# Top-k attention and a low-rank mixer on one core: rounding passes spread over the fills, transposes of the second batch moved, an inverse moved

## The chip, the cores and the metric

One core of one Trainium2 chip. The metric is the device time of one execution in microseconds (us). The core has five engines with a queue each, which work through their instructions in order and wait for each other by semaphores: TensorE (PE, with its weight loads PEld), VectorE (DVE), ScalarE (ACT), GpSimd (POOL) and SyncE (SP), which issues the transfers.

## The reference

Attention over 8 batches x 8 heads, 576 rows, 64 columns a head; in each row of scores only the 32 largest stay. Its output, put together over the heads, goes through a mixer: a low-rank mix over the rows and a two-layer product over the channels.

```python
scores = scale * np.matmul(q, k.transpose(0, 1, 3, 2))
kth = np.partition(scores, -top_k, axis=-1)[..., -top_k:-top_k + 1]
scores = np.where(scores >= kth, scores, -1000000000.0)
attn = np.exp(scores - np.max(scores, axis=-1, keepdims=True))
attn = attn / (np.sum(attn, axis=-1, keepdims=True) + 1e-09)
x = np.matmul(attn, v)                    # then to (8, 576, 512)
h = x.transpose(0, 2, 1) @ U @ V
u = x + h.transpose(0, 2, 1)
out = u + np.maximum(u @ w_ch1, 0.0) @ w_ch2
```

U, V and the two weight matrices come in 64-bit floats; the kernel makes 32-bit ones of them on the chip.

## The kernel before

**Pairs and steps.** Two heads of a batch are a pair: 4 pairs a batch, 32 in all. A pair's 576 rows are cut into four blocks of 128 rows (for both heads, in two "chunks" of 576 scores) and a tail of 64 rows (both heads in one chunk). A block is a step: 5 steps a pair, 20 a batch, 160 in all, numbered n = 0 to 159, with g = n // 5 the pair and t = n % 5 (t = 4 is the tail). The order on PE, ACT, DVE and POOL is written out by hand: what the Python loop issues first stands first in the queue.

**What happens to one block.** `scores` (L271) makes the scores on PE and ACT copies them to `Ssb` (L305 to L307, three buffers). `front` (L327) is a generator that is moved on by `next`: four rounds on DVE find the 32 largest (L346 the first eight, then L356 blanks what was found and L360 finds eight more; a step begins with L346). Then the chunk is masked and `E = exp` is made, on one of three ways (`ways`, L314):

- early: ACT makes exp before the mask, DVE masks and sums with L366;
- pooled: POOL makes a mask (L363) and adds it to the scores (L364), then ACT makes exp with its sum (L312);
- gaps: ACT makes a relu of the distance to the least kept score (L380, L381), POOL subtracts it (L382), then ACT makes exp (L312).

In batches 0 and 1 (pairs 0 to 7) a step has a gaps chunk and, but for tails, a pooled chunk; `eased` says so. Those steps take three `next(last)` in the step after. From pair 8 on there is an early and a pooled chunk. The end of batch 0 (pair 3) has its own ways.

`turns` (L391) transposes a block's `E` on PE: four transposes of the first chunk, four of the second (L402), one for the last columns (L407), each group into a buffer `tp` and copied by ACT to `PT` (L403, L408). There are two `tp` buffers, shared with all other short PE results (`O`, `pT`, `up`, the transposes of q, k and of the output). `values` (L417) multiplies with v into `O`; ACT copies it to `XT` (L448). The sums `den` are inverted on DVE (L414, L415) by `inverse` (L411).

**The mixer.** When a pair is complete, `mixed` (L451, a generator too) turns `XT` back (L460), ACT copies it (L464), POOL multiplies with the inverted sums (L465); after `wait` further fills PE makes `pT` (L471), ACT copies `Tb`, and PE makes `up` (L483, L485), which ACT copies into `uT` (L493). After the last pair of a batch it appends that batch's products, `mlp(b)` (L498), to `fillers`. Over the eight batches these are 1024 products on each of two lines, each product in two passes on PE: L508 from `uT` to `hT` (ACT's relu L520), L527 from `hT` to the output columns, of which ACT makes `oT` (L542), POOL adds `uT` (L543), PE turns it back (L555), and SP stores it. The last of these turns is issued as soon as the batch's products run out (L546).

**Fills.** The products of a batch are dealt out over the 20 steps that follow. `fill` (L582) moves `mixing` on by one, adds a share to `due` and issues products until `due` is used up; if there are none, `due` is set to 0. A step has 8 fills. In batch 0 there is nothing to fill in; what is left at the end runs alone.

**The weights.** 36 layers of raw 64-bit words are loaded by `next_params` (L205). For each, ACT runs three passes over the raw words (L165, L167, L168: Copy with a scale, Identity with a scale and bias, Sign); at the call after, DVE shifts (L175) and POOL adds twice (L176, L178). A call joins the layer of the call before, runs the passes of the next, and starts a load. It is called up to twice a step, until about step 28.

## Time and profile before

| | us |
|---|---|
| median of 4 runs | 1846.93 (1846.5 to 1847.78) |
| the profiled execution, its own time | 1846.5 |
| its span, first to last instruction | 1843.7 |
| PE busy | 1740.1 (94%), 10528 matmuls |
| DVE busy | 1570.6 (85%) |
| ACT busy | 1015.4 (55%) |
| POOL busy | 684.4 (37%) |
| products on PE, L508 and L527 | 557.1 and 562.3 |
| DVE's rounds, L346, L356, L360 | 205.0, 211.7 + 427.7, 614.7 |

Spans and waits are from the profiled execution. A line of a timeline gives the start, the duration, the engine, the source line, the operation with the tiles it writes and reads, and in brackets how long its engine sat idle before it and what released it. A line of the list of waits gives the waiting engine and line, what it waited for, and then the total in us, the number of times and the longest. Since the kernel changes its bottleneck on the way (DVE alone in batch 0, products on PE beside attention after that, products alone at the end), the busy shares are read by stretches.

### The profile page before, as it was taken

How to read it: one execution, taken by the hardware profiler on the slowest of the kernel's cores; microseconds unless marked ns; L12 is line 12 of the kernel's file. 1: busy time of each engine (PE TensorE's matmuls, PEld its weight loads, DVE VectorE, ACT ScalarE, POOL GpSimd, SP SyncE). 2: the span in 40 equal slices, each digit the busy share in tenths (PEclk: the TensorE clock that was granted, in tenths of full speed). 3: DMA queues.
4: the chain of work that ended last, by engine and by line, in shares of the span. 5: the costliest groups of instructions: out<-in, count | busy, mean ns of one | idle time of the engine just before them, and what ended most of it. 6: DMA issues, size and time to landing. Idle time of an engine off the chain costs nothing.

```text
span 1843.7 us, 29145 instructions
## 1 busy us (share of the span) xinstructions
PE 1740.1 (94%) x10528; PEld 1316.8 (71%) x10528; DVE 1570.6 (85%) x3208; ACT 1015.4 (55%) x2518; POOL 684.4 (37%) x471
## 2 busy tenths in 40 slices
PE   4656889999999999999999999999999999999999
PEld 2344656787778877787777877788777877778677
DVE  7999998999999999998999999999999999996000
ACT  5787777665546555555555555555555555454110
POOL 4777577453333223423233233323223333332000
PEclk7777899999999999999999999999999999999999
DMA  4232221101010000111010010110001010000000
GB/s 109 78 89 84 66 77 47 31 24 29 20 28 23 22 20 20 32 25 31 15 27 17 24 29 21 30 25 24 19 17 31 21 32 19 10 8 7 6 15 12
DMA packets 127294, 58.20 MB, mean 32 GB/s; under 512 B 89904, under 2 KB 124976, under 8 KB 127152
## 3 DMA queue, kind: packets, MB, share of 16 engines
q1 hardware_dynamic: 126096, 56.10, 11.5%
q8 instruction: 83, 1.36, 0.3%
q14 instruction: 59, 0.48, 0.1%
q10 hardware_dynamic: 1056, 0.26, 0.1%
HBM read 46.89 MB, written 9.44 MB: 31 GB/s over the span
## 4 chain that ended last, share of the span: by engine, by line
PE 84%; DVE 10%; POOL 3%; ACT 2%; issue 1%; DMA 0%; SPq 0%; POOLq 0%; DVEq 0%; ACTq 0%
PE mm L508 26%; PE mm L527 26%; PE sc L294 7%; PE O L439 6%; PE tp L402 6%; DVE rr L356 4%; DVE m L360 3%; PE sc L281 2%; PE O L426 2%; PE up L483 2%; PE O L436 1%; DVE first L346 1%; PE tp L266 1%; PE tp L555 1%; PE up L485 1%
## 5 line engine op out<-in xcount | busy, mean ns | idle before, releaser
L360 DVE MAX8 m<-rr 128x8 f32<-128x576 f32 x864 | 614.7, 748 | 5.5
L527 PE MATMUL mm<-hT,w 128*128 128x256 f32 (+1 forms) x2048 | 562.3, 410 | 0.0
L508 PE MATMUL mm<-uT,w 128*128 128x256 f32 (+1 forms) x2048 | 557.1, 410 | 1.8 <-ACT hT L520 1.8
L363 POOL TENSOR_SCALAR E<-Ssb,m 128x576 f32<-128x576 f32 x127 | 284.0, 2236 | 564.1 <-DVE m L360 405.9
L508 PEld LDWEIGHTS mm<-uT,w 128*128 128x128 f32 x2048 | 363.4, 190 | 108.3 <-issue 27.6
L527 PEld LDWEIGHTS mm<-hT,w 128*128 128x128 f32 x2048 | 360.5, 190 | 97.7 <-issue 22.5
L356 DVE MATCH_REPLACE8 rr<-m,rr 128x576 f32<-128x576 f32 x576 | 427.7, 742 | 0.0
L403 ACT COPY PT<-tp 128x512 f32<-128x512 f32 x288 | 168.4, 587 | 127.2 <-PE tp L402 126.2
L312 ACT ACTIVATE E<-Ssb,nmax 128x576 f32<-128x576 f32 x288 | 223.0, 775 | 26.4 <-POOL Ssb L364 16.3
L346 DVE MAX8 first<-Ssb 128x8 f32<-128x576 f32 x288 | 205.0, 748 | 17.4 <-ACT Ssb L307 17.4
L356 DVE MATCH_REPLACE8 rr<-first,Ssb 128x576 f32<-128x576 f32 x288 | 211.7, 742 | 0.0
L402 PE MATMUL tp<-ident,E 128*128 128x128 f32 x1152 | 178.0, 279 | 35.4 <-ACT E L312 14.2
L402 PEld LDWEIGHTS tp<-ident,E 128*128 128x128 f32 x1152 | 141.5, 143 | 86.9 <-ACT E L312 24.6
L364 POOL TENSOR_TENSOR Ssb<-Ssb,E 128x576 f32<-128x576 f32 x127 | 179.5, 1413 | 10.6
L294 PE MATMUL sc<-qkT 64*128 64x288 f32 x1024 | 168.5, 449 | 12.0 <-ACT Ssb L305 7.9
L366 DVE SCALAR_TENSOR_TENSOR E<-Ssb,m,E 128x576 f32<-128x576 f32 x122 | 109.3, 896 | 73.5 <-ACT E L312 62.7
L520 ACT ACTIVATE hT<-mm 128x320 f32<-128x320 f32 (+1 forms) x256 | 104.2, 407 | 118.1 <-PE mm L508 117.7
L439 PE MATMUL O<-PT,va 128*64 128x128 f32 x2048 | 145.2, 286 | 0.0
L448 ACT COPY XT<-O 128x128 f32<-128x128 f32 x128 | 34.1, 267 | 176.6 <-PE O L439 176.5
L543 POOL TENSOR_TENSOR oT<-oT,uT 128x320 f32<-128x320 f32 (+1 forms) x56 | 44.5, 795 | 225.9 <-ACT oT L542 205.2
L294 PEld LDWEIGHTS sc<-qkT 64*128 64x128 f32 x1024 | 91.9, 195 | 50.2 <-issue 16.2
L439 PEld LDWEIGHTS O<-PT,va 128*64 128x64 f32 x2048 | 113.5, 141 | 16.1 <-issue 1.3
(80 smaller groups left out, 1554.9 us busy)
## 6 DMA issues: line engine op xcount, KB each, us to landing
raw<-in_moe_w_ch_dram SPq DMA_DIRECT2D x32, 512.0 KB, 3.7
va<-in_v_dram SPq DMA_DIRECT2D x64, 128.0 KB, 2.3
out_dram<-ob SPq DMA_DIRECT2D x64, 128.0 KB, 1.9
ld_q<-in_q_dram SPq DMA_DIRECT2D x63, 128.0 KB, 2.8
ld_k<-in_k_dram SPq DMA_DIRECT2D x63, 128.0 KB, 2.7
ld_ends<-in_q_dram SPq DMA_DIRECT2D x32, 32.0 KB, 2.1
ld_ends<-in_k_dram SPq DMA_DIRECT2D x32, 32.0 KB, 2.2
vd<-in_v_dram SPq DMA_DIRECT2D x64, 16.0 KB, 2.0
```

The source lines that it names most:

```text
L294: nc.tensor.matmul(sc[:, h, 0:HALF], lhsT=qkT[half(h), 0, cols(t)], rhs=qkT[half(h), 1, i * HALF : (i + 1) * HALF], start=True, stop=True,)
L312: nc.scalar.activation(E, chunk, AF.Exp, bias=nmax, scale=SCALE, accum_out=total)
L346: nc.vector.max(ms[c], curs[c])
L356: nc.vector.match_replace(nxt, ms[c], curs[c], NEG)
L360: nc.vector.max(ms[c], curs[c])
L363: nc.gpsimd.tensor_scalar(Es[c], chunks[c], ms[c][:, 7:8], NEG, ALU.is_lt, ALU.mult)
L364: nc.gpsimd.tensor_tensor(chunks[c], chunks[c], Es[c], ALU.add)
L402: nc.tensor.transpose(tp[:, j, :], E2[:, a : a + P], ident)
L403: nc.scalar.copy(PT[:, NT * h : NT * h + NT], tp)
L439: nc.tensor.matmul(O[half(h)], lhsT=va[:, h, j, :], rhs=PT[:, NT * h + j], start=False, stop=(j == NT - 1),)
L508: nc.tensor.matmul(ph[:, 0:w], lhsT=w1[:, cc, f * P : (f + 1) * P], rhs=uT[:, cc, lo:hi], start=(cc == 0), stop=(cc == NC - 1),)
L527: nc.tensor.matmul(po[:, 0:w], lhsT=w2[:, f, c * P : (c + 1) * P], rhs=hTs[f][:, 0:w], start=(f == 0), stop=(f == NF - 1),)
```

## The change

Four edits, all of them to the order in which things are issued; no instruction is added or left out.

1. `f64_parts` no longer runs ACT's three passes but puts them into a list `passes`. Each `fill` runs one, before it moves `mixing` on; what is left is run at the head of the next `next_params`.
2. At n = 19, the last step of batch 0, `inverse` is called after the tail's rounds instead of before the last two of them.
3. Where the block of step n - 1 is eased (steps 21 to 40), its first group of transposes is no longer issued at the end of step n, but with the two others in step n + 1: one after the first fill, two after the second.
4. In steps after batch 0, `mixed` waits 5 fills instead of 4.

```diff
@@ f64_parts
-        nc.scalar.activation(bits.bitcast(F32), hi.bitcast(F32), AF.Copy, scale=RESCALE)
-        lows = low.bitcast(F32)
-        nc.scalar.activation(lows, low8, AF.Identity, bias=four[0:n], scale=-(1 + 2.0**-10) * 2.0**-26)
-        nc.scalar.activation(hi.bitcast(F32), hi.bitcast(F32), AF.Sign, bias=nudge[0:n])
+        lows, his = low.bitcast(F32), hi.bitcast(F32)
+        passes.extend((
+            lambda: nc.scalar.activation(bits.bitcast(F32), his, AF.Copy, scale=RESCALE),
+            lambda: nc.scalar.activation(
+                lows, low8, AF.Identity, bias=four[0:n], scale=-(1 + 2.0**-10) * 2.0**-26
+            ),
+            lambda: nc.scalar.activation(his, his, AF.Sign, bias=nudge[0:n]),
+        ))
@@ next_params
+        while passes:
+            passes.pop(0)()
         while parts:
             f64_join(*parts.pop(0))
@@ fill
         for _ in range(k):
+            if passes:
+                passes.pop(0)()
             if mixing and next(mixing[0], True):
                 mixing.pop(0)
@@ the loop, n = 19
             if n < ALONE:
+                next(here)
+                next(here)
                 inverse(g, 0, 2 * NT)
-                next(here)
                 mixing.append(mixed(g, 1))
                 fill()
-                next(here)
                 next(here)
                 continue
@@ the loop, from n = 21 on
         next(turning, None)
         fill()
         next(turning, None)
+        if eased(*divmod(n - 2, CH)):
+            next(turning, None)
         fill()
         next(ready, None)
...
         if n - 2 >= ALONE and (n - 2) % CH == NT:
-            mixing.append(mixed((n - 2) // CH, 4))
+            mixing.append(mixed((n - 2) // CH, 5))
...
         if n <= STEPS:
             turning = turns(*divmod(n - 1, CH))
-        next(turning, None)
+        if not ease:
+            next(turning, None)
         fill()
```

## The prediction

> **What bounds the kernel now.** I read the page first, then the busy times cut at the steps of the loop (a step starts where DVE begins a new `L346`), then PE's waits in each stretch, then the timeline around every wait that this change can touch.

> The page: slices of 46 us, tenths busy.

> ```profile
> span 1843.7 us, 29145 instructions
> PE   4656889999999999999999999999999999999999
> DVE  7999998999999999998999999999999999996000
> ...
> L268 ACT ACT_TABLE_LOAD x1 | 1.3, 1283 | 2.1 <-issue 2.1
> ```

> DVE is full first, PE from slice 7 on, and the last three slices are PE alone. (The third row, from ScalarE's list of groups, is used below.) The same in stretches that end at steps 20, 30, 40 and so on; columns are PE, PEld, DVE, ACT and POOL busy, then the granted clock.

> ```profile
> 11.30:209.00 197.70, 121.99 (x744) 81.15 (x743) 192.12 (x393) 147.54 (x355) 138.36 (x101) 0.75 0.29 83
> 209.00:317.40 108.40, 97.08 (x571) 67.24 (x571) 97.78 (x199) 81.90 (x197) 78.54 (x55) 1.00 0.23 68
> 317.40:416.00 98.60, 98.60 (x643) 78.12 (x642) 89.99 (x182) 65.39 (x175) 47.31 (x31) 1.00 0.11 26
> 628.00:840.60 212.60, 211.76 (x1318) 161.73 (x1317) 197.66 (x407) 115.70 (x288) 68.79 (x44) 1.00 0.10 24
> ```

> Steps 0 to 18 are DVE's (0.07 us idle in most steps); in steps 20 to 29 PE is idle 11.3 us and DVE 10.6 us, each waiting for the other through ScalarE and GpSimd; from step 30 PE is never idle but for 0.83 us a batch. So after 317 us only PE's waits count, before it what makes PE late. PE's waits in 209 to 318 us, then in 470 to 1690 us, and DVE's in 198 to 470 us (total, times, longest):

> ```profile
> PE tp L402 <- ACT E L312: 4.8, 3, 1.9
> PE mm L508 <- ACT hT L520: 1.8, 1, 1.8
> PE pT L471 <- POOL x L465: 1.2, 1, 1.2
> ...
> PE tp L555 <- POOL oT L543: 4.1, 5, 0.8
> ...
> DVE first L346 <- ACT Ssb L307: 16.5, 6, 5.0
> DVE den L414 <- ACT E L312: 3.1, 1, 3.1
> ```

> Two places in the timeline: step 29, where DVE waits for ScalarE, ScalarE for GpSimd, and PE for ScalarE; and the end of a batch's products in step 62.

> ```profile
> 313.76 1.40 POOL L382 TENSOR_TENSOR Ssb<-Ssb,E 128x576 f32<-128x576 f32 x1
> 315.19 0.77 ACT L312 ACTIVATE E<-Ssb,nmax 128x576 f32<-128x576 f32 x1 [0.49 <-POOL Ssb L382]
> 316.11 0.66 PE L402 MATMUL tp<-ident,E 128*128 128x128 f32 x4 [1.94 <-ACT E L312]
> 317.39 1.42 DVE L346 MAX8 first<-Ssb 128x8 f32<-128x576 f32 x2 [5.00 <-ACT Ssb L307]
> ...
> 655.47 0.37 ACT L542 COPY oT<-mm 128x256 f32<-128x256 f32 x1 [0.49 <-PE mm L527]
> 655.92 0.72 POOL L543 TENSOR_TENSOR oT<-oT,uT 128x256 f32<-128x256 f32 x1 [3.60 <-ACT oT L542]
> 656.70 0.44 PE L555 MATMUL tp<-ident,oT 128*128 128x128 f32 x2 [0.83 <-POOL oT L543]
> 658.85 1.24 PE L294 MATMUL sc<-qkT 64*128 64x288 f32 x8
> ```

> **1. The passes dealt out.** The number of instructions stays (36 of each, 0.67 to 0.78 us for a full layer); only ScalarE's order changes. In steps 0 to 18 DVE waits for nothing of ScalarE's and the score copies stand almost a step ahead of their use, so I take 0. If that cover went, each step could lose up to one pass, 0.75 us. In steps 20 to 29 there are two effects. A gain: the relu that frees PE's product buffer no longer stands behind three passes; of the 1.8 us wait some 1.2 go. A loss: GpSimd's `L176` needs the third pass, and in steps 23 and 28 its order puts that pass behind an `hT` or `ob` copy. The chain L176, L178, L363, L364, L382, `L312`, `L307` that ends in DVE's 5.00 us wait then starts about 0.6 and 0.75 us later. A loss of 1.35 us on DVE's side, bounds 0 and 2 x 1.5.

> [...]

> **2. The inverse behind the rounds.** DVE's `L414` waits 3.1 us at step 19 with the tail's rounds queued behind it (`L356`, `L360`, then all of step 20). The two remaining rounds take 4 x 0.75 to 0.83 us = 3.2 us, which is when the sums are there. DVE starts step 20 at about 205.9 instead of 209.0. What waits for `den` is GpSimd's `L465`, not before 210.3, so that costs nothing. PE's chain at that place (it runs through `uT`, `O`, `PT` copies) gains only some 0.7 us, from the `uT` copy that stood behind three passes. So DVE's 3.1 us are no end gain by themselves; of them I let 2.0 reach step 29: 3.1 less the 0.6 of part 1, less 0.5 since PE, 0.7 us earlier, has only its 1.5 us wait in step 22 to give. Bounds 0 and 3.1.

> **3. The second batch's transposes.** In steps 21 to 40 the first four transposes leave the end of a step, where three of them waited 4.8 us in all for an `E` just being made, for the next step's start. But nothing DVE waits for is bought by that: its 5.00 us are ScalarE standing at `L312` for GpSimd. And the new place has its own waits. There are two buffers `tp`. The last transpose (`L407`) now follows the second four at once and takes the first four's buffer, so it needs their copy (`L403`, 0.59 us), which on ScalarE stands behind `L380` and `L381` (0.2 + 0.78 us), and those behind DVE's last round. `values` then waits for one copy more: 0.6 us later in step 29 (309.55 + 0.27 before). Before step 30: 1.94 us wait gone, less 0.6, plus the 2.0 of part 2, less 0.44 for four transposes only put off: PE is 2.9 us ahead at step 30. Bounds 0.3 and 6.5 (all three waits gone, 4.8, and 1.7 more).

> From step 30 PE is full, and each new wait counts. With a fill between, the copy has 1.0 to 1.5 us and needs about 0.9: I charge 0.1 us in ten of twelve steps. In steps 32 and 37 `up` comes directly after `L407` and needs the copy of the second four, started only as they end: 0.3 + 0.59 - 0.1 = 0.8 us each. Together 2.6 us lost; bounds 0 and 12 x 0.9 = 10.8.

> **4. `mixed` waits a fill longer.** The 1.2 us wait of `pT` goes, inside the stretch counted above. From batch 2 on nothing waited there; the new order leaves at least 0.85 us between `pT` and `up` where the copy of `Tb` ends 0.6 us after the last `pT` starts (703.7 to 704.3 us in batch 2): 0, bounds 0 and 24 x 0.2 = 4.8. Past step 42 it does something unmeant. The next batch's products are appended when `mixed` ends, one fill later; in step 42 nothing else is left, so that fill issues none. All later products slip by one fill (about 0.97 of a 512-column product, about 0.9 us of PE work, which is put off, not added). A batch's products therefore end in the fill after `values` and `scores` instead of before. The `oT` of the last rows is made at the same place; `L555` comes 1.3 + 1.24 us of PE work later. The five waits of 0.83 us have nothing left to wait for: 4.1 us gained. Bounds 0 and 5 x 1.0. One `oT` add per batch also falls behind `L363` and `L364` on GpSimd (2.2 + 1.4 us), but its reader comes most of a step later. The waits of step 42 and of the last batch (1.3 us each) stay.

> [...] Weight loads are 161.7 of 212.6 us here, which would leave room to swallow the 4.1 us; but the timeline's products start every 0.22 us (256 columns) and 0.27 us (320) without a break, so I count them.

> **Sum**, against this execution: -2.9 + 2.6 - 4.1 = -4.4 us, span 1839.3. The execution took 1846.5 us with 2.8 us around the span; the median of the four is 1846.93, so I predict **1842.5 us**. The bounds together: best -6.5 - 5 = -11.5, worst -0.3 + 10.8 + 4.8 = +15.

> **Rivals.**
> - *B, given back.* The waits of part 3 eat the start's gain, or the scores' copies on ScalarE delay `oT`, so that part 4 only moves its wait: one of the two gains stays, -1.5 to -3 us, about 1845. For it: ScalarE is in order and busy 82 of 108 us. Against: PE gets 2.5 us of work in between, where 0.83 us is missing.
> - *C, slower.* `L407`'s buffer. If the first four's copy comes 1.2 us later than I think in each of steps 30 to 41, PE loses 12 x 1.2 = 14.4 us, of which -2.9 - 4.1 pay 7.0: +7.4, 1854. It is slower at all from 0.58 us a step. Against: `L380` runs early in the step there, and ScalarE is idle 3 us a step.
> - *D, more.* DVE's and PE's waits of steps 20 to 29 go together and nothing comes back: -6.5 - 4.1 = -10.6, 1836.3.
> - That the change does not do what it says is no rival for the order (the built programs show the instructions moved as written), but the products' slip is not in its name.

> **Chances.** Forecast 0.52, B 0.20, C 0.15, D 0.13. A measurement of this kernel can tell about 0.2%, 3.7 us, from no change. My forecast lies just beyond that: 0.42 of its 0.52 is faster than 1843.2, 0.10 within. With D: faster 0.55. Within: 0.10 + B + 0.02 of C = 0.32. Slower 0.13. The range 1835 to 1851 leaves out the far ends of C and D.

> **What would show it.** Right: DVE's wait at `L414` gone and step 20 at 206; PE's waits for `E` gone; `L555` waiting twice instead of seven times; batches 212.4 us apart becoming about 211.6; DVE still idle 4 to 5 us in steps 24 and 29. Wrong: PE waits on `PT` or `Tb` copies between 318 and 430 us of more than 3 us; any PE wait in steps of batch 2 and later; a batch still taking 212.4 us.

## The result and the profile after

The changed kernel takes 1843.5 us (median of 37 runs, 1842.11 to 1844.81) where the kernel before takes 1846.76 us (median of 57 runs shown with them): 3.3 us less, a ratio of 0.9982 with a 95% interval of 0.9977 to 0.9987. The prediction was 1842.5 us. The profiled execution spans 1840.8 us where that of before spanned 1843.7. Line numbers of the changed kernel are 1 to 6 higher than those of before: `L175` is now `L179`, `L346` is `L352`, `L402` is `L408`, `L407` is `L413`, `L520` is `L526`, `L555` is `L561`.

The page of the changed kernel, span and the two rows of busy tenths in slices of 46 us:

```profile
span 1840.8 us, 29144 instructions
PE   4666889999999999999999999999999999999999
DVE  7999988989999999999999999999999999995000
```

Its busy times in the same stretches, cut at its own steps 20, 30 and 40 and at one batch (PE, PEld, DVE, ACT, POOL busy, then the granted clock, DMA share, GB/s):

```profile
11.30:205.60 194.30, 122.32 (x719) 81.20 (x718) 191.93 (x393) 145.58 (x351) 138.43 (x101) 0.72 0.30 85
205.60:315.35 109.75, 101.94 (x604) 70.92 (x603) 97.01 (x199) 83.89 (x201) 78.47 (x55) 1.00 0.22 67
315.35:415.64 100.29, 98.25 (x637) 77.31 (x636) 89.99 (x182) 65.03 (x175) 47.25 (x31) 1.00 0.10 26
627.60:839.80 212.20, 211.93 (x1320) 162.57 (x1319) 196.42 (x407) 117.32 (x290) 68.35 (x44) 1.00 0.10 24
```

Step 20 starts 3.4 us earlier (205.60, before 208.99), step 30 only 2.0 (315.35, before 317.39), step 40 0.4 (415.64, before 416.01). From there each batch of 20 steps takes 211.74 us (839.41 to 1051.15) instead of 212.37, five times 0.63.

PE's waits in 205 to 318 us (total, times, longest), those of 0.4 us and more:

```profile
PE tp L413 <- ACT PT L409: 6.2, 6, 3.0
PE tp L408 <- ACT E L318: 0.4, 1, 0.4
PE pT L477 <- ACT x L440: 0.4, 1, 0.4
PE O L442 <- ACT PT L414: 0.4, 1, 0.4
```

One of the six waits at `L413`, 0.6 us, lies in step 30 already, the other five (5.6 us) before it. PE's waits in 318 to 470 us; from 470 to 1690 us the view lists none any more, where before it listed five of 0.83 us:

```profile
PE tp L561 <- POOL oT L549: 1.3, 1, 1.3
PE up L489 <- ACT PT L409: 1.1, 2, 0.6
PE tp L561 <- ACT PT L409: 0.2, 1, 0.2
```

The waits for `E` (4.8 us before), `hT` (1.8) and `x` from GpSimd (1.2) are gone or small; in their place PE waits 6.2 us at the last transpose, `L413`, for the copy that frees its buffer. DVE's waits in 195 to 470 us: the one at the sums is gone, the one for the score copies is longer than before (19.8, before 16.5):

```profile
DVE first L352 <- ACT Ssb L313: 19.8, 8, 5.8
DVE E L372 <- ACT E L318: 3.9, 2, 2.3
DVE w L179 <- ACT w L167: 1.1, 2, 0.6
```

The longest new wait, in the timeline of step 25 (start, length, engine, what, idle before):

```profile
260.25 0.69 ACT L167 ACTIVATE w<-raw 128x512 f32<-128x512 f32 x1
260.38 0.60 PE L408 MATMUL tp<-ident,E 128*128 128x128 f32 x4
260.83 0.75 ACT L168 ACTIVATE raw<-raw,four 128x512 f32<-128x512 uint8 x1
261.48 0.75 ACT L171 ACTIVATE raw<-raw,nudge 128x512 f32<-128x512 f32 x1
262.12 0.19 ACT L386 ACTIVATE least<-m 128x1 f32<-128x1 f32 x1
262.34 0.77 ACT L387 ACTIVATE E<-Ssb,least 128x576 f32<-128x576 f32 x1
263.02 0.42 ACT L526 ACTIVATE hT<-mm 128x320 f32<-128x320 f32 x1
263.34 1.06 ACT L409 COPY PT<-tp 128x512 f32<-128x512 f32 x2
263.97 0.33 PE L413 MATMUL tp<-ident,E 128*128 128x128 f32 x1 [2.99 <-ACT PT L409]
```

ScalarE is never idle here. Ahead of the copy that PE needs stand the three rounding passes that part 1 dealt to the first fills, then `L386`, `L387` and a relu: part 1 and part 3 meet in ScalarE's queue. (Part 3 has such waits without part 1 too; see its run alone.) And the end of a batch's products, in step 62: the add is done at 657.63, the transposes start at 658.76 behind `scores`, and wait for nothing:

```profile
656.45 0.37 ACT L548 COPY oT<-mm 128x256 f32<-128x256 f32 x1 [0.49 <-PE mm L533]
656.56 0.85 PEld L445 LDWEIGHTS O<-PT,va 128*64 128x64 f32 x16
656.90 0.73 POOL L549 TENSOR_TENSOR oT<-oT,uT 128x256 f32<-128x256 f32 x1 [5.07 <-ACT oT L548]
657.59 1.24 PE L300 MATMUL sc<-qkT 64*128 64x288 f32 x8
658.76 0.44 PE L561 MATMUL tp<-ident,oT 128*128 128x128 f32 x2
```

**Where PE's time went.** For each PE instruction I took the spacing to the next start, less the median spacing of its shape, and added that up by stretches; this is PE time lost. From the first product to PE's last instruction the granted clock is 1.00 in both profiles, so none of it is the clock's. From 216 us (the first product) to 316: 16.5 us before, 13.75 after, -2.7. From 316 to 440: 6.05 and 8.67, +2.6. From 440 to the end: 67.06 and 64.38, -2.7. Together -2.8, the difference of the two executions from the first product on (1627.6 and 1624.8 us).

### The profile page after: what moved, and what is told of

Its sections match the earlier page's. It is cut to its first block, busy times and chain, and to the rows that moved or that the text cites. A ratio compares the mean times of both kernels' runs of the same rounds, so it can differ in the third digit from the quotient of the medians.

```text
span 1840.8 us, 29144 instructions
## 1 busy us (share of the span) xinstructions
PE 1745.1 (95%) x10528; PEld 1322.7 (72%) x10528; DVE 1561.3 (85%) x3208; ACT 1021.8 (56%) x2518; POOL 682.0 (37%) x471
## 3 DMA queue, kind: packets, MB, share of 16 engines
q1 hardware_dynamic: 126096, 56.10, 11.5%
## 4 chain that ended last, share of the span: by engine, by line
PE 83%; DVE 9%; ACT 5%; POOL 2%; issue 1%; DMA 0%; SPq 0%; POOLq 0%; ACTq 0%; DVEq 0%
PE mm L533 26%; PE mm L514 25%; PE sc L300 7%; PE O L445 6%; PE tp L408 6%; DVE rr L362 4%; DVE m L366 3%; PE sc L287 2%; PE O L432 2%; PE up L489 2%; PE O L442 1%; PE tp L272 1%; ACT E L318 1%; DVE first L352 1%; PE up L491 1%
## 5 line engine op out<-in xcount | busy, mean ns | idle before, releaser
L352 DVE MAX8 first<-Ssb 128x8 f32<-128x576 f32 x288 | 205.2, 749 | 20.7 <-ACT Ssb L313 20.7
L362 DVE MATCH_REPLACE8 rr<-first,Ssb 128x576 f32<-128x576 f32 x288 | 211.8, 742 | 0.0
L408 PE MATMUL tp<-ident,E 128*128 128x128 f32 x1152 | 177.7, 279 | 31.4 <-ACT XT L454 11.9
L408 PEld LDWEIGHTS tp<-ident,E 128*128 128x128 f32 x1152 | 141.6, 143 | 81.5 <-ACT E L318 16.4
L526 ACT ACTIVATE hT<-mm 128x320 f32<-128x320 f32 (+1 forms) x256 | 104.9, 410 | 141.8 <-PE mm L514 140.5
L370 POOL TENSOR_TENSOR Ssb<-Ssb,E 128x576 f32<-128x576 f32 x127 | 179.7, 1415 | 10.6
L372 DVE SCALAR_TENSOR_TENSOR E<-Ssb,m,E 128x576 f32<-128x576 f32 x122 | 100.9, 827 | 78.2 <-ACT E L318 67.5
```

Of the source, the lines that this page charges most:

```text
L352: nc.vector.max(ms[c], curs[c])
L362: nc.vector.match_replace(nxt, ms[c], curs[c], NEG)
L370: nc.gpsimd.tensor_tensor(chunks[c], chunks[c], Es[c], ALU.add)
L408: nc.tensor.transpose(tp[:, j, :], E2[:, a : a + P], ident)
```

## Experiments

All are timed beside the kernel before on the same chip, in five rounds (5 to 11 executions of each kernel, 9 to 29 of the one before); the difference is that of the medians, then the ratio's interval. "Parts" are the prediction's: 1 the passes, 2 the inverse, 3 the transposes, 4 the longer wait of `mixed`. The "slip" is what part 4 does besides: all products behind step 42 are issued one fill later.

| kernel | us | before | difference | ratio, 95% |
|---|---|---|---|---|
| part 1 alone | 1846.96 | 1846.80 | +0.2 | 0.9993 to 1.0011 |
| part 2 alone | 1843.75 | 1846.80 | -3.05 | 0.9976 to 0.9993 |
| part 3 alone | 1848.44 | 1846.80 | +1.6 | 0.9999 to 1.0017 |
| part 4 alone | 1842.69 | 1847.10 | -4.4 | 0.9971 to 0.9989 |
| the slip alone | 1843.99 | 1847.10 | -3.1 | 0.9978 to 0.9996 |
| part 4 without the slip | 1841.37 | 1847.10 | -5.7 | 0.9959 to 0.9982 |
| parts 2, 4 | 1839.73 | 1846.87 | -7.1 | 0.9950 to 0.9975 |
| parts 1, 2, 4 | 1843.62 | 1847.10 | -3.5 | 0.9973 to 0.9990 |
| parts 2, 3, 4 | 1842.37 | 1846.35 | -4.0 | 0.9971 to 0.9989 |
| all, part 3 only in steps 21 to 30 | 1839.96 | 1846.80 | -6.8 | 0.9950 to 0.9977 |
| the same, last oT handed on | 1837.60 | 1846.87 | -9.3 | 0.9935 to 0.9962 |
| the same, score copies first | 1835.28 | 1846.87 | -11.6 | 0.9924 to 0.9949 |

Of each kernel one execution was profiled, and a single profile is good for the length of a stretch rather than for a point in time. The kernel before, part 4 alone, the slip alone and part 4 without the slip have the same order up to the first product, and it starts at 216.13, 214.23, 215.81 and 216.25 us in their profiles.

### Part 4: is it the slip?

Part 4 alone:

```diff
-            mixing.append(mixed((n - 2) // CH, 4))
+            mixing.append(mixed((n - 2) // CH, 5))
```

> The kernel before with part 4 alone (mixed waits five fills). Theory (the products' slip): the five waits of PE for oT at the batch ends vanish, batches 0.63 us shorter as in the changed kernel (212.37 to 211.74), 5 x 0.63 = 3.1 us less; the pT wait of 1.2 us in step 27 goes too, but PE may only meet it again at the next E (0 to 1.2 us): 1842.5 to 1843.7 us. Rival (part 4 alone moves its waits, the batches' gain needs the other parts): 1846 to 1847 us, batches 212.4 us.

1842.69 us, batches 211.74 us apart, no PE wait from 470 to 1690 us: the batches' gain needs no other part.

The slip alone, `mixed` still waiting four fills:

```diff
         if gi == NPAIR - 1:
+            if b == 1:
+                yield
             fillers.append(mlp(b))
```

> The kernel before, mixed still waiting four fills; only the products of the second batch are appended one fill later in step 42, so that all later products slip by a fill and pT, up and Tb stand where they stood. Theory (slip): the gain of the batches is all here, batches 211.5 to 211.8 us, 1843 to 1844 us. Rival (the gain comes from pT and up standing a fill later): batches 212.4 us, 1846.5 to 1847 us.

1843.99 us, batches 211.95 us apart, none of the five waits. The slip is enough to remove them, and brings 0.42 of the 0.63 us a batch. Is it needed? Wait of five fills, with the share of the empty fills kept:

```diff
                 if not fillers:
-                    due = 0.0
+                    if n < 2 * ALONE + 2:
+                        due = 0.0
                     break
```

> The kernel before with mixed waiting five fills, but the share of work of the empty fills of step 42 and after is kept, so the products catch up and do not slip; a batch's last transposes stand before values again, with the second up (one 256-column product and two transposes, some 0.65 us of PE) now ahead of them. Theory (slip, as the prediction has it: without it no gain): batches 212.4 us, 1845.6 to 1847 us. Rival (the later up pads the 0.83 us wait): waits of about 0.2 us, batches 211.7 us, 1843 to 1844 us.

1841.37 us, batches 211.70 us apart: the rival is right. PE's waits from 470 to 1690 us in this kernel:

```profile
PE tp L555 <- POOL oT L543: 0.9, 5, 0.2
```

Five waits of 0.2 us instead of 0.83: the second `up` now stands between the last product and `L555` and pads the wait. Either move does it; the slip is one of two, and by the medians not the better one. Without it the wait before the last batch is 0.7 us, not 1.3 as in part 4 alone; the rest of the 1.3 us between the two medians no wait explains.

### Parts 1 to 3, alone and together

The changed kernel with part 3 taken back:

```diff
-        if eased(*divmod(n - 2, CH)):
-            next(turning, None)
...
-        if not ease:
-            next(turning, None)
+        next(turning, None)
```

> The changed kernel with part 3 undone (parts 1, 2 and 4 stay). Theory (the prediction's terms): steps 30 to 41 lose nothing, 2.6 us less; before step 30 the moved transposes' share (0.9 of the 2.7 us gained) is missing; about 1841.7 us, PE waiting for E again before step 30 and not for PT in steps 30 to 41. Rival (part 3 is what lets PE use the 3 us of part 2, since PE otherwise stands before E longer): no gain before step 30, 1843.5 us, the same as the changed kernel.

1843.62 us, as the rival said; whether for the rival's reason, the wait for `E`, is looked at below. Which of parts 1, 2 and 4 is in the way it does not tell; the next runs take the parts singly. Part 3 alone, on the kernel before:

```diff
+        if eased(*divmod(n - 2, CH)):
+            next(turning, None)
...
-        next(turning, None)
+        if not ease:
+            next(turning, None)
```

> The kernel before with part 3 alone. Theory 1 (the prediction's terms): the waits of PE for E go, waits for copies of PT come; about 0.9 us gained before step 30 and 2.6 us lost in steps 30 to 41, batches still 212.4 us: about 1848.5 us. Theory 2 (the clock): the 1.9 us wait of PE in step 29 is what lets the granted clock fall to about a half for some 3.4 us after it in the runs of part 4 alone and of the slip alone (316 to 320 us, 1.7 us lost); with that wait gone no low clock near step 30, another 1.7 us less in the runs that had it: about 1846.8 us.

1848.44 us, the number of theory 1, though the interval just reaches no change. In its trace the waits for `E` are gone before step 30 and PE waits 5.5 us for copies of `PT` at `L407` (the longest 2.1) and 3.2 us for `hT` instead; in steps 32 and 37 `up` waits 1.1 us in all. As theory 2 says the clock does not fall near step 30 (1.00 from 216 to 382 us), but in the profile of the kernel before it does not either (1.00 there too); the gain it expected from that did not show.

Part 2 alone:

```diff
-                inverse(g, 0, 2 * NT)
                 next(here)
+                next(here)
+                inverse(g, 0, 2 * NT)
                 mixing.append(mixed(g, 1))
                 fill()
                 next(here)
-                next(here)
```

> The kernel before with part 2 alone. Theory (the prediction's): DVE starts step 20 3.1 us earlier, PE's chain to step 24 does not, so the waits of DVE and PE between step 20 and 29 only change place: 1846.5 to 1847 us, with PE's E wait of step 29 shorter by what DVE keeps (2 us or more of DVE kept would leave none). Rival (DVE's 3.1 us reach the end, at least 2.0 of them): 1844 to 1845 us.

1843.75 us: the rival. DVE starts step 20 at 206.04 and step 30 at 315.11, 2.3 us ahead of before, and PE's wait for `E` in step 29 is 1.95 us, exactly as long as before: PE stands there for a thing that DVE's chain makes, so what DVE gains PE gains. (The profiled execution, 1846.01 us, is the slowest of the eleven; what it loses behind step 30 stands in the last section.)

Part 1 alone is the change's first hunks, of which the core is

```diff
+            if passes:
+                passes.pop(0)()
             if mixing and next(mixing[0], True):
```

> The kernel before with part 1 alone. Theory (the prediction's): nothing in batch 0, the 1.8 us wait of PE for hT falls to about 0.6, DVE's chain in steps 23 and 28 about 1.35 us later; in all within 0.7 us of the kernel before. Rival (a pass at every fill delays the score copies, so that DVE waits in steps 0 to 19): step 20 starts 2 us or more later, 1848.5 us or more.

1846.96 us: nothing, as the theory said. The wait for `hT` fell from 1.8 to 0.5 us; but PE's wait for `E` in step 29 grew from 1.9 to 3.2. PE was ahead and met the same `E`, and steps 20 to 30 of DVE took 109.06 us (108.40 before).

Parts 2 and 4, the two that gain alone, are the diffs of both together:

> The kernel before with parts 2 and 4. Alone they measured -3.05 and -4.4 us; with part 1 as a third (the changed kernel without part 3) the sum was only -3.5. Theory A (it is part 1 that costs, since it sets PE ahead only to wait 3.2 us for E in step 29 with the granted clock at a half for 6 us after it): the two add, -6 to -7.5 us, 1839.5 to 1841 us, PE's wait for E in step 29 about 2 us. Theory B (2 and 4 are in each other's way): 1843 to 1844 us, the wait for E in step 29 3 us or more and a clock of a half behind it.

Theory A: 1839.73 us, -7.1, where the two parts alone add to -7.5. So part 1 on top of them costs 3.6 us (the fourth run's -3.5). The two traces show where such a cost arises. PE's waits from 300 to 318 us with parts 2 and 4 (total, times, longest):

```profile
PE tp L402 <- ACT E L312: 2.2, 1, 2.2
```

The same view with parts 1, 2 and 4:

```profile
PE tp L408 <- ACT E L318: 3.2, 1, 3.2
```

And the join on GpSimd ahead of step 29's chain, with the third pass that it needs, in the timeline with parts 2 and 4, where the step starts at 302.96 us:

```profile
302.96 0.75 ACT L168 ACTIVATE raw<-raw,nudge 128x512 f32<-128x512 f32 x1
303.79 1.30 POOL L176 TENSOR_TENSOR w<-w,raw 128x512 uint32<-128x512 uint32 x1 [1.03 <-ACT raw L168]
```

The same with parts 1, 2 and 4, where the step starts at 303.83 us:

```profile
304.23 0.59 ACT L409 COPY PT<-tp 128x512 f32<-128x512 f32 x1
304.70 0.79 ACT L171 ACTIVATE raw<-raw,nudge 128x512 f32<-128x512 f32 x1
305.57 1.30 POOL L180 TENSOR_TENSOR w<-w,raw 128x512 uint32<-128x512 uint32 x1 [1.96 <-ACT least L386]
```

With the passes dealt out the third one stands behind the copies of `ob` and `PT`, and the join starts 1.75 us into the step instead of 0.8. The step is longer by as much (11.66 us, 10.74), and step 24 by 0.6 (10.90, 10.33): DVE takes 109.80 us from step 20 to 30 (205.69 to 315.49) instead of 108.29 (205.41 to 313.70). `E` is later by as much against step 20, and PE waits 1.0 us longer for it.

The longer wait has a second price, which the expectation named: the granted clock behind it (the column before the last two). With parts 1, 2 and 4 it is a half from 313.20 to 320.03 us:

```profile
313.20:316.62 3.42, 2.40 (x7) 1.92 (x8) 1.13 (x2) 3.29 (x10) 0.88 (x2) 0.50 0.02 5
316.62:320.03 3.41, 3.41 (x10) 2.41 (x9) 3.41 (x9) 0.91 (x2) 1.41 (x1) 0.50 0.00 0
```

With parts 2 and 4 it stays whole:

```profile
311.27:314.69 3.42, 2.26 (x12) 1.74 (x13) 0.98 (x2) 3.15 (x10) 1.03 (x2) 1.00 0.02 5
314.69:318.10 3.41, 3.41 (x26) 2.61 (x25) 3.41 (x9) 2.50 (x6) 1.41 (x1) 1.00 0.00 0
```

PE is busy 5.81 us at half speed, 2.9 us lost, and steps 30 to 40 take 101.39 us (315.49 to 416.87) instead of 98.55 (313.70 to 412.25). Since the clock differs between executions of one kernel (its mean is 0.970 to 0.977 in the five of parts 2 and 4) and only one of each is profiled, how much of the 3.6 us between the medians is the later `E` and how much the clock is not shown.

The last run takes part 1 off the changed kernel:

```diff
-            if passes:
-                passes.pop(0)()
             if mixing and next(mixing[0], True):
```

> The changed kernel with part 1 undone (parts 2, 3 and 4 stay). Parts 2 and 4 together measured -7.1 us; with part 1 added -3.5; parts 1 and 3 alone +0.2 and +1.6. Theory A (part 1 holds up GpSimd's L176 and so DVE, and with it PE's E, in the whole change too): 1840 to 1841.5 us, and DVE needs 108.3 to 109 us from step 20 to 30 where the changed kernel needs 109.75. Theory B (part 1 costs only where part 3 is away; with part 3 the copies of PT wait behind the passes anyway): 1843 to 1844 us, steps 20 to 30 within 0.3 us of 109.75.

1842.37 us lies between the two theories. DVE took 108.93 us from step 20 to 30, as theory A said (109.75 in the changed kernel), but PE then waits 5.8 us for copies of `PT` at `L407`, so little of it is left: -4.0 against -3.3 us for the whole change, with intervals that overlap. Part 3 costs 3.1 us on top of parts 2 and 4, part 1 costs 3.6, and the two together 3.8, hardly more than one. That each puts PE or DVE behind the same `E` of step 29 or the copies before it would explain this, but no run separates it from the clock. How much part 1 costs within the whole change stays open between 0 and about 1.5 us.

### What a better version keeps

Part 3 only up to step 30:

```diff
-        if eased(*divmod(n - 2, CH)):
+        if eased(*divmod(n - 2, CH)) and n <= ALONE + 10:
             next(turning, None)
...
-        if not ease:
+        if not ease or n >= ALONE + 10:
             next(turning, None)
```

> The changed kernel with part 3 only in steps 21 to 30; from then on the first four transposes stand at the end of a step again. Theory: the losses of steps 30 to 41 (two waits of 0.73 us excess in steps 32 and 37, 0.36 at the oT transposes of step 39, some 0.1 us each elsewhere) go, the rest stays: 1.5 to 2.6 us less than the changed kernel, 1841 to 1842 us. Rival (the losses of steps 30 to 41 are the slower start of the second half whatever the order, because E or DVE is late there): 1843.5 us.

1839.96 us, more than expected. Steps 30 to 40 take 97.74 us (315.96 to 413.70) instead of 100.29, 2.55 less, and PE's only wait from 318 to 470 us is 1.3 us for `oT`. The other us between the medians is not explained by a wait.

A batch's last `oT` transposes handed to the next batch (its fourth `hT` runs them):

```diff
+    late = []
+
     def mlp(b):
 
         uT = uTs.pop(b)
-        late = []
...
-        late.pop()()
+        if b == B - 1:
+            late.pop()()
```

> The changed kernel with part 3 only in steps 21 to 30 and a batch's last oT transposes handed to the next batch's fourth hT (only the last batch still does its own at once). Theory: the two PE waits for oT that are left (1.3 us in step 42 and 1.3 us before the last batch) go: 1.5 to 2.6 us less than with the first half alone (1839.96), 1837.4 to 1838.5 us. Rival (what PE does instead meets its own wait, as the last product's buffer): 1840 us.

1837.6 us, the theory: 2.4 us less than with the first half alone. Step 42 takes 10.87 us instead of 12.34. Last, the score copies ahead of the `E` that waits for GpSimd, in the tail steps 24 and 29:

```diff
-        if ease:
+        if ease and (t < NT or n >= ALONE + 10):
             next(last, None)
...
             scores(*divmod(n + 1, CH))
+        if ease and t == NT and n < ALONE + 10:
+            next(last, None)
```

> The same, and in the tail steps 24 and 29 the score copies stand ahead of ScalarE's E that waits for GpSimd. Theory (DVE's waits for Ssb in steps 24 and 29, 4.2 and 6.1 us, are ScalarE's order and are worth time): step 30 starts 3 to 5 us earlier, PE's waits before it get shorter by part of that: 1834 to 1836.5 us. Rival (PE's place at step 30 is set by its own waits for PT copies): step 30 earlier for DVE, the time the same as without it, 1837 to 1838.5 us.

1835.28 us, 11.6 us less than before and 2.3 less than without this last edit: the theory. Step 30 starts at 310.56. DVE's waits in 203 to 318 us, 5.5 us for the score copies where without the edit it was 11.5 and in the kernel before 9.0 (in 205 to 318):

```profile
DVE first L352 <- ACT Ssb L313: 5.5, 4, 2.0
DVE w L179 <- ACT w L167: 1.5, 2, 0.9
```

The prediction named this order on ScalarE as the cause of DVE's 5.00 us wait and left it there; the run shows that an edit can take part of it.

## Why the prediction was right, and where its steps were not

**The total.** -4.4 us was predicted, -3.3 measured in the medians and -2.9 in the spans. The three terms of the sum, against PE's lost time: the start -2.9 predicted and -2.7 found, steps 30 to 41 +2.6 and +2.6, the batches -4.1 and -2.7. For the batches and for steps 30 to 41 the mechanism was the one named; the term that is most out in size is part 4's. That the start came out as forecast is luck: what its sum was made of did not happen so, as parts 1 to 3 below show.

**Part 4.** "The five waits of 0.83 us have nothing left to wait for: 4.1 us gained" is right about the waits and too large by 0.2 us a batch: PE meets small waits that were covered (for `E` twice, 0.06 and 0.09 us; for the `tp` buffer ahead of `pT`, 0.12 us behind the copy of `ob`), priced at 0. Five times 0.63 is 3.1; and between 440 and 628 us 0.75 us more is lost than before (10.6 against 9.9), in the same small waits. That the waits of step 42 and of the last batch stay was right (1.3 us each). The slip as the cause was right for this kernel, but not the only way to the gain, as the kernel without it shows.

**Part 3.** "1.94 us wait gone, less 0.6" before step 30: the waits for `E` did go, nearly all 4.8 us, and what took their place was about ten times what I wrote, 6.2 us at `L413` in six steps. I named the buffer and its copy behind ScalarE's queue, and priced it at 0.6 from one step, 29, where the queue is short. In step 25 the passes of part 1 are in that queue too, and the wait is 3.0 us; but the price was wrong for the order of before as well, since part 3 alone has 5.5 us of these waits and the changed kernel without part 1 has 5.8. That the whole of part 3 came out at +1.6 alone (+2.8 in its profile, from the first product on), where my terms make +1.7 (-0.9 and +2.6), is luck in part: two misjudged pieces that nearly cancel before step 30 and one that was right after it: `up` in steps 32 and 37 lost 0.73 us each (0.8 predicted).

**Part 2.** DVE's step 20 at 205.6 (205.9 predicted), `L414`'s wait gone. "No end gain by themselves" is wrong: alone it is worth 3.05 us, in its profile 2.3 at step 30. That is so because PE's wait for `E` in step 29 is a wait for DVE's chain and moves with it: 1.95 us long as before, but 2.3 us earlier. The 2.0 that the sum let through was nearly the size.

**Part 1.** The gain on `hT` and the delay of the join were both there (1.3 and 1.5 us; 1.2 and 1.35 predicted), and alone they cancel. But the gain is PE's and the loss is DVE's: PE's is lost again at the next `E`, and DVE's is not. With part 2's gain on DVE the loss counts, and in the profile of parts 1, 2 and 4 the clock adds to it (a half from 313.20 to 320.03 us, 2.9 us lost). The sum set only 0.6 of the 1.35 us against part 2's gain and gives no reason for leaving out the rest. ScalarE loads its table once in the changed kernel as it did before (1.3 us, the third row of the page in the prediction, now `L274`): the passes between its exps and relus brought no further load.

**Rivals.** B asked whether only one of the two gains stays; the batches' did and the start's was paid for by steps 30 to 41, which is the forecast. C's delay of 1.2 us a step came in step 25 (3.0 us) before step 30, not in the full steps after it, where the waits on `PT` copies total 1.9 us (0.6 in step 30, 1.1 for `up`, 0.2 at `L561`).

## What to carry to other kernels

An engine that stands before a product of another engine's chain gained nothing here by arriving earlier (part 1 alone): price an edit first by which side of that wait it moves. When a change has several parts on one in-order queue, price each against the queue as all of them leave it, and run each part alone and with one left out; here two parts were worth 7.1 us of which the other two took 3.8. The short wait at the end of a batch went away with either of two pieces of work put between producer and consumer; look for the nearest work before moving a schedule. And where single executions differ by as much as the edit, read a cause from the length of a stretch in the trace, and look at the clock in it.

## What the runs showed of the hardware that was not expected

```profile
310.87:314.28 3.41, 3.30 (x28) 1.98 (x24) 1.49 (x2) 0.52 (x2) 3.33 (x3) 1.00 0.00 0
314.28:317.69 3.41, 1.58 (x9) 1.26 (x10) 0.30 (x1) 2.92 (x10) 1.70 (x2) 1.00 0.02 5
317.69:321.11 3.42, 3.42 (x18) 2.53 (x16) 3.42 (x8) 2.71 (x7) 1.42 (x1) 1.00 0.00 0
```

Part 2 alone:

```profile
311.32:314.73 3.41, 1.46 (x9) 0.88 (x8) 0.00 (x0) 2.68 (x7) 2.38 (x3) 1.00 0.00 0
314.73:318.14 3.41, 3.41 (x11) 2.31 (x10) 3.03 (x7) 1.80 (x6) 1.42 (x1) 0.50 0.02 5
```

Before, the idle time is split, 0.11 us in one stretch and 1.83 in the next, and the clock stays at 1.00. With part 2 alone all 1.95 us lie in one stretch, and in the next PE is busy throughout at half speed: 1.7 us lost. Steps 30 to 40 take 100.31 us with part 2 alone and 98.62 before. The 3.0 us wait of step 25 left the clock at 1.00 in the changed kernel, split 1.39 to 1.60:

```profile
258.96:262.37 3.41, 2.02 (x13) 1.37 (x11) 2.06 (x5) 3.38 (x11) 1.66 (x2) 1.00 0.08 23
262.37:265.78 3.41, 1.81 (x8) 1.34 (x9) 3.38 (x10) 2.60 (x7) 2.22 (x2) 1.00 0.38 130
265.78:269.20 3.42, 3.42 (x31) 2.41 (x30) 3.39 (x7) 2.70 (x10) 1.76 (x2) 1.00 0.12 36
```

The kernel with part 3 only up to step 30 has the same wait there, 3.02 us, with 2.51 us of idle time in one stretch, and a clock of half behind it:

```profile
260.41:263.82 3.41, 0.90 (x4) 0.74 (x5) 3.41 (x9) 3.11 (x8) 1.41 (x1) 1.00 0.46 154
263.82:267.24 3.42, 3.42 (x16) 2.46 (x17) 3.38 (x9) 1.49 (x4) 2.57 (x2) 0.50 0.00 0
```

The eleven times of part 4 alone lie in two groups, 1842.4 to 1842.7 and 1843.7 to 1844.3, and those of parts 2, 3 and 4 at 1841.8 to 1842.4 and 1843.4 to 1843.8: a gap of about the size of one such loss. But both profiled executions (1842.52 and 1841.85 us) are of the faster group and hold such a stretch themselves, from 314.97 and from 230.10 us, so that the groups are this effect is not shown.
